# Attention and a mixture of experts in one kernel: sums of the first expert moved to GpSimd, and the tasks around the border of the two parts placed anew

## The chip, the cores and the metric

The kernel runs on one core of one Trainium2 chip. Its time is device microseconds of that core. A core has five engines that work side by side, each through its own queue of instructions in order: TensorE (PE, matrix multiplications into PSUM; PEld is its load of the stationary operand), VectorE (DVE), ScalarE (ACT), GpSimd (POOL) and SyncE (SP, which only issues DMAs here). They wait for each other through semaphores.

## The reference, cut to what matters

```python
def _attn_ref(q, k, v):                      # batch 8, heads 8, seq 576, head_dim 64
    scores = scale * np.matmul(q, k.transpose(0, 1, 3, 2))
    bias = slopes[:, None, None] * (-np.abs(rel).astype(np.float32))[None, :, :]
    mask = (rel >= 0) & (rel < window)       # window 128
    scores = np.where(mask, scores + bias[None], -1000000000.0)
    attn = np.exp(scores - np.max(scores, axis=-1, keepdims=True))
    attn = attn / (np.sum(attn, axis=-1, keepdims=True) + 1e-09)
    return np.matmul(attn, v)

def _moe_ref(x, w_gate, w1, w2):             # N 4608, D 512, E 8 experts, F 1024
    logits = x @ w_gate
    expert_idx = np.argmax(logits, axis=1)
    gate_w = softmax(logits)[arange(N), expert_idx]
    for e in range(E):                       # over the rows of expert e
        y[rows] = np.maximum(x[rows] @ w1[e], 0.0) @ w2[e]
    return gate_w[:, None] * y
```

The output of the attention, laid out as 4608 rows of 512, is the x of the second part. All is float32.

## The kernel before

**Attention.** The batch is cut into 4 pairs of sequences (bp) and each pair into 4 pairs of heads (hp): 16 units u. A unit has four groups g of key blocks (GR); the main loop runs over the 64 groups i. `scores(i)` (L762) makes a group's products on PE (L769), takes the exponential on ACT (L775) and multiplies with the bias factors on DVE (L778, L783); the result is `prob[i]`. `values` (L792, L804) multiplies it with v, `finish` (L812) copies the result into `xT` (L821, L823) and makes the sums of the softmax on PE (L836), which DVE adds to `sumT` (L847). A constant AHEAD = 3 sets how many groups the scores are ahead of the values. Loads of the unit after next are paced by small DMAs that wait for a `prob` (L640).

**Routing.** When a pair's four units are done, a list of tasks (`behind`, L1309) is worked off, one entry at each call of `some()` (one per group): `gate` and `turn` make the logits and bring tokens to partitions; `scale_a` to `scale_c` make the softmax scales, the choice of expert and `es`, the factor of each row and head (L952); `count` and `place` number the tokens of each expert (PE L967, L969); `ones_at`, `ones_at2` and `enlist` (L1000 to L1033) build the table of tokens through one-hot matrices. The rows, unscaled, and their scales go to `x_rows` in memory (`row_out`, or `squares_turned` and `squares_out` where DVE turns 32x32 squares; POOL puts the scales in, L1099, then DMAs, L1108). After the third pair, `early_table` numbers the first 512 tokens of expert 0, and `gather` (L1230, POOL) reads them back. The last pair's list is made by `with_tail` (L1607) and worked off inside the first layer of expert 0.

**Experts.** Groups run in a list: expert 0, expert 1, then further tiles and experts in turn. `prepare` (L1288) makes for each of an expert's four tiles a `to_scale` (DVE, L1252) and a `to_columns` (L1254; for experts 0 and 1 turned on PE, L1265, and copied by ACT, L1266), then sums. The two layers (`strassen1` L1415, `strassen2` L1496) use seven products M1 to M7 (ORDER: 1, 2, 6, 5, 7, 3, 4) in place of eight, each in two halves of 8 matmul records. M1 and M2 need no sums and only tiles 0 and 1; M6, M5 and M4 need sums of x (`xs`, four DVE instructions, L538 to L541) or of w1 (`ws`, L530 to L533); the second layer needs eight sums of w2 (`w2s`) and sums of the hidden layer (`hs`). After each half `step()` issues one entry of the list `fill`, so that list sets where the instructions of tasks stand on every engine, PE's queue among them. `drain(g)` issues what is left of a group's entries before its layer ends.

**The border.** In the last unit, expert 0's `prepare` is added to the tasks at its first group, so tiles 0 to 2 are scaled and turned inside the unit and tile 3 and the x sums just behind. `with_tail` has 13 entries. In expert 0's second layer stand the gather for expert 1, `count_all`, `check_all`, `table_further`, `next_groups` (values loaded from `xe` into registers) with `pieces` "1", `pieces` "2" (PE L1142, which waits for DVE's `index`), and then the whole of `prepare(fixed[1])`. The weights of expert 1 (L1587, L1588) go where the attention's rows lay, and so wait for the last DMAs out of them.

The lines that set how far the scores are ahead:

```python
        AHEAD = 3
        for i in range(AHEAD):
            scores(i)
...
            if i + AHEAD < NG:
                scores(i + AHEAD)
```

## Time and profile before

| what | us |
|---|---|
| median of 3 runs (731.38 to 735.25) | 732.21 |
| the profiled execution | 691.06 |
| its span, first to last instruction | 689.2 |
| mean granted TensorE clock | 0.985 |

Busy time by stage, from the view by stretches of time:

| stretch, us | what runs | PE busy | DVE busy | ACT busy | POOL busy | PE clock |
|---|---|---|---|---|---|---|
| 0 to 20 | first unit and a half | 11.86 | 8.90 | 9.80 | 17.09 | 1.00 |
| 168 to 181 | end of attention | 9.86 | 5.43 | 4.13 | 4.57 | 0.87 |
| 181 to 205 | expert 0, first layer, with the last pair's tasks | 23.36 | 17.96 | 7.61 | 1.33 | 1.00 |
| 205 to 220 | its end and the start of the second layer | 14.33 | 14.69 | 3.61 | 0.00 | 1.00 |
| 219 to 233 | second layer, M6 and M5 | 10.46 | 9.22 | 0.74 | 4.26 | 0.88 |
| 233 to 245 | second layer, M7 to M4 | 12.00 | 6.54 | 3.46 | 3.29 | 1.00 |

How to read it: an engine with less busy time than the stretch is long waited, or had nothing to do. PE is the only one that is nearly full over the whole span, so the question at each place is what PE waits for. In a timeline, the number in brackets is the idle time just before the instruction, and behind the arrow stands what ended it. A PE clock below 1.00 means that part of the stretch ran at half rate.

### The profile page before, as it was taken

What the parts mean: (1) busy time and instruction counts of PE and PEld (TensorE: products, weight loads), DVE (VectorE), ACT (ScalarE), POOL (GpSimd) and SP (SyncE); (2) the same over time, 40 slices, a digit from 0 to 9 for tenths busy, and PEclk for the clock granted to TensorE, in tenths of its full rate; (3) what the DMA queues carried; (4) which work ended last, traced back from release to release, by engine and by line L of the source; (5) the groups of instructions that cost most, each with busy time, mean ns of one, the idle gap of its engine ahead of it and who ended that gap; (6) DMA issues with size and microseconds to landing.
All of it is one profiled execution on the core that took longest, in us unless ns stands there. A gap on an engine that the chain in (4) does not pass through costs nothing.

```text
span 689.2 us, 14460 instructions
## 1 busy us (share of the span) xinstructions
PE 655.8 (95%) x6004; PEld 548.2 (80%) x6004; DVE 379.4 (55%) x717; ACT 199.2 (29%) x365; POOL 237.6 (34%) x360
## 2 busy tenths in 40 slices
PE   5899889998999899999999999999999999999996
PEld 4778768687687788878897887888788978878893
DVE  4567769786489476614842564275148435633500
ACT  5555446465331223113202310231131123002210
POOL 8100572215001176117323702652172247023020
PEclk9999899999999999999999999999999999999999
DMA  9677987854516964185448237652844573284010
GB/s 285 200 222 192 287 241 219 289 157 149 165 22 162 386 206 140 57 292 170 155 154 301 57 129 258 212 166 63 296 137 145 178 276 97 86 305 154 1 62 8
DMA packets 63549, 122.00 MB, mean 177 GB/s; under 512 B 5905, under 2 KB 30001, under 8 KB 63474
## 3 DMA queue, kind: packets, MB, share of 16 engines
q1 hardware_dynamic: 51778, 92.78, 42.0%
q0 software_dynamic: 10544, 27.31, 12.4%
q8 instruction: 49, 0.80, 0.5%
q10 hardware_dynamic: 1152, 0.88, 0.4%
q14 instruction: 26, 0.21, 0.1%
HBM read 101.79 MB, written 19.96 MB: 177 GB/s over the span
## 4 chain that ended last, share of the span: by engine, by line
PE 75%; issue 9%; DVE 8%; DMA 4%; POOL 2%; ACT 1%; SPq 0%; POOLq 0%; DVEq 0%; ACTq 0%
PE sp L769 5%; PE at L804 5%; PE pair0b L1511 4%; PE pair0a L1511 4%; PE pair0b L1454 4%; PE pair0a L1454 4%; PE pair1a L1511 4%; PE pair1b L1511 4%; PE pair2b L1454 4%; PE pair1b L1454 4%; PE pair1a L1454 4%; PE pair2a L1454 4%; PE pair2a L1511 4%; PE pair2b L1511 4%; PE m L836 3%
## 5 line engine op out<-in xcount | busy, mean ns | idle before, releaser
L1240 POOL DMA_INDIRECT xg<-x_rows,p_idx x124 | 125.0, 1008 | 37.8 <-issue 37.5
L1534 POOL DMA_INDIRECT out_dram<-zo,s_idx x39 | 44.5, 1140 | 250.6 <-DVE zo L1525 149.6
L769 PE MATMUL sp<-q_sb,k_sb 64*64 64x192 f32 (+2 forms) x1152 | 60.2, 331 | 7.1 <-DMA q_sb<-in_qT_dram 6.9
L775 ACT ACTIVATE pe<-sp 128x768 f32<-128x768 f32 x64 | 51.9, 811 | 49.6 <-PE sp L769 46.7
L804 PE MATMUL at<-pe,v_sb 64*64 64x192 f32 (+2 forms) x1408 | 59.6, 289 | 3.4 <-issue 3.4
L778 DVE TENSOR_TENSOR pe<-pe,fac 128x768 f32<-128x768 f32 x48 | 45.5, 952 | 28.3 <-ACT pe L775 27.8
L804 PEld LDWEIGHTS at<-pe,v_sb 64*64 64x64 f32 x1408 | 48.0, 138 | 9.5 <-issue 6.9
L769 PEld LDWEIGHTS sp<-q_sb,k_sb 64*64 64x64 f32 x1152 | 42.0, 141 | 16.6 <-DMA q_sb<-in_qT_dram 4.3
L1465 ACT ACTIVATE h<-h 128x512 f32<-128x512 f32 x32 | 20.2, 631 | 41.3 <-DVE h L1464 41.3
L836 PE MATMUL m<-pe,ind 128*32 128x192 f32 (+2 forms) x704 | 29.8, 288 | 0.6 <-issue 0.6
L1252 DVE TENSOR_TENSOR xn<-xg 128x512 f32<-128x512 f32 x39 | 26.3, 676 | 3.4 <-DMA xg<-x_rows,g_idx 3.1
L836 PEld LDWEIGHTS m<-pe,ind 128*32 128x32 f32 x704 | 23.2, 110 | 3.0 <-issue 1.0
L1108 POOL DMA_DIRECT2D x_rows<-xs x40 | 21.6, 548 | 6.4 <-POOL xs L1099 1.9
L783 DVE TENSOR_TENSOR pe<-pe,fac 128x768 f32<-128x768 f32 x16 | 15.3, 955 | 15.2 <-ACT pe L775 15.1
L1268 DVE STREAM_TRANSPOSE xgT<-xn 128x512 f32<-128x512 f32 x31 | 22.1, 712 | 1.1
L538 DVE TENSOR_TENSOR w2s<-w 128x512 f32<-128x512 f32 x16 | 10.9, 684 | 19.4 <-DMA w<-in_moe_w_dram 19.4
L1099 POOL COPY xs<-sq 128x16 f32<-128x16 f32 x10 | 2.6, 258 | 53.8 <-ACT sq L1081 53.8
L1566 PE MATMUL pair2a<-w,h 128*128 128x512 f32 x48 | 21.1, 592 | 0.0
L821 ACT COPY xT<-at 128x640 f32<-128x640 f32 (+1 forms) x32 | 18.7, 585 | 6.5 <-PE at L804 4.6
L1454 PE MATMUL pair0b<-xgT,w 128*128 128x256 f32 x72 | 17.2, 382 | 0.0
L1511 PE MATMUL pair1a<-w,h 128*128 128x256 f32 x72 | 17.0, 379 | 0.0
L1454 PE MATMUL pair0a<-xgT,w 128*128 128x256 f32 x72 | 17.0, 379 | 0.0
(375 smaller groups left out, 1393.2 us busy)
## 6 DMA issues: line engine op xcount, KB each, us to landing
w<-in_moe_w_dram SPq DMA_DIRECT2D x29, 2048.0 KB, 7.9
k_sb<-in_kT_dram SPq DMA_DIRECT2D x15, 576.0 KB, 5.6
q_sb<-in_qT_dram SPq DMA_DIRECT2D x15, 576.0 KB, 5.6
v_sb<-in_v_dram SPq DMA_DIRECT2D x30, 288.0 KB, 4.5
x_rows<-xs POOLq DMA_DIRECT2D x16, 264.0 KB, 3.8
x_rows<-xs POOLq DMA_DIRECT2D x32, 66.0 KB, 4.7
x_rows<-xT SPq DMA_DIRECT2D x8, 264.0 KB, 5.2
w<-in_moe_w_dram SPq DMA_DIRECT2D x4, 512.0 KB, 7.7
```

The source lines that it names most:

```text
L769: nc.tensor.matmul(sp[c * KB : (c + 1) * KB, r, c0 : c0 + n], lhsT=k_sb[u][hs, c, kb * KB : (kb + 1) * KB], rhs=q_sb[u][hs, c, kb * KB : k ...
L775: nc.scalar.activation(pe[:], sp[:, :, :GC], AF.Exp, scale=SCALE)
L778: nc.vector.tensor_tensor(pe.rearrange("p r (k c) -> p r k c", k=2), pe.rearrange("p r (k c) -> p r k c", k=2), fac[:, h0 : h0 + 2, None, ...
L804: nc.tensor.matmul(acc[r * D : (r + 1) * D, c, lo - q0 : hi - q0], lhsT=v_sb[u][c * KB : (c + 1) * KB, kb, r * D : (r + 1) * D], rhs=pe[c ...
L836: nc.tensor.matmul(sm[32 * j : 32 * j + 32, lo - q0 : hi - q0], lhsT=none[:] if pe is None else ind[:, hp, :], rhs=fac[:, 0, :KB] if pe is ...
L1108: eng.dma_start(x_d[r0 : r0 + n * m, a * PW : (a + 1) * PW].rearrange("(k i) w -> i k w", i=TQ), xs[a * TQ : (a + 1) * TQ, p0 // TQ : p0 / ...
L1240: nc.gpsimd.indirect_dma_start(out=to, out_offset=None, in_=where, in_offset=bass.IndirectOffsetOnAxis(ap=idx, axis=0),)
L1252: nc.vector.tensor_tensor(xn[:], x, s.unsqueeze(3).to_broadcast([P, NA, HP, TQ]), op=ALU.mult)
L1268: nc.vector.transpose(to.rearrange("p h (k j) -> p k h j", j=TQ), xn[:])
L1454: nc.tensor.matmul(ps[:, f * 256 : (f + 1) * 256], lhsT=left[m][:, d, fb * P : (fb + 1) * P], rhs=right[m][:, d, :], start=(m in (1, 2, 5) ...
L1511: nc.tensor.matmul(ps[:, :256], lhsT=left[m][:, f, c * P : (c + 1) * P], rhs=right[m][:, f, :], start=(m in (1, 2, 5) and f == 0), stop=Tr ...
L1534: ins = nc.gpsimd.indirect_dma_start(out=out[:, :], out_offset=bass.IndirectOffsetOnAxis(ap=s_idx[:, g["c0"] + j : g["c0"] + j + 1], axis= ...
```

## The change

It has five parts.

1. `scores_to` takes the place of AHEAD: two groups ahead in units 0 and 1, three from unit 2 on.
2. Expert 0: `prepare` is added to the tasks one group later, and only its first three entries (tile 0 scaled; tile 0 turned with tile 1 scaled; tile 1 turned with tile 2 scaled). The others, `first[3]` to `first[8]`, stand in `with_tail`: tile 2 is turned after M1's first half, tile 3 after its second. Expert 1 likewise: tiles 0 and 1 are turned in expert 0's second layer, tiles 2 and 3 and the x sums in its own first layer.
3. The four x sums of expert 0 and its eight w2 sums run on POOL, all placed after M1's second half; before, on DVE, the w2 sums spread over the second half of the first layer and the start of the second.
4. The last pair's tasks: `scale_a2` and `scale_b2` have entries of their own, `ones_at` and `ones_at2` come one half later, the one-hot columns are taken from `oc_of`, `squares_scaled` (POOL's copies) stands apart from `squares_out` and is done for all nine tiles at once, and tile 8 goes out through POOL's DMA queue and no longer through SP's.
5. The numbering of the third pair: `early_holes` apart and one entry earlier, the table and the gather with `enlist`. In the second layer `next_groups` and `pieces` "1" have entries of their own.

```diff
@@ -533,12 +533,12 @@
                 lambda: eng.tensor_tensor(s4, a12, s2, op=ALU.subtract),
             ]
 
-        def sums_t(b11, b12, b21, b22, t1, t2, t4):
+        def sums_t(b11, b12, b21, b22, t1, t2, t4, eng=nc.vector):
             return [
-                lambda: nc.vector.tensor_tensor(t1, b12, b11, op=ALU.subtract),
-                lambda: nc.vector.tensor_tensor(t2, b22, t1, op=ALU.subtract),
-                lambda: nc.vector.tensor_tensor(b12, b22, b12, op=ALU.subtract),
-                lambda: nc.vector.tensor_tensor(t4, b21, t2, op=ALU.subtract),
+                lambda: eng.tensor_tensor(t1, b12, b11, op=ALU.subtract),
+                lambda: eng.tensor_tensor(t2, b22, t1, op=ALU.subtract),
+                lambda: eng.tensor_tensor(b12, b22, b12, op=ALU.subtract),
+                lambda: eng.tensor_tensor(t4, b21, t2, op=ALU.subtract),
             ]
 
         def w1_sums(g, eng=nc.vector):
...
@@ -1080,23 +1080,29 @@
                 half = slice(r * KB, (r + 1) * KB)
                 nc.scalar.copy(sq[half].rearrange("p t k h -> p k t h"), ps5[half, :, :, r, :])
 
+        def squares(bp, t):
+            if (bp, t) not in xs_of:
+                if bp in spare and t < TPB - 1:
+                    w = NA * PW
+                    flat = spare[bp].rearrange("p h n -> p (h n)")
+                    xs_of[bp, t] = flat[:, t * w : (t + 1) * w].rearrange("p (k w) -> p k w", k=NA)
+                else:
+                    xs_of[bp, t] = rows.tile([P, NA, PW], F32, name="xs")
+            return xs_of[bp, t]
+
         def squares_turned(bp, t):
-            if bp in spare and t < TPB - 1:
-                w = NA * PW
-                flat = spare[bp].rearrange("p h n -> p (h n)")
-                xs = flat[:, t * w : (t + 1) * w].rearrange("p (k w) -> p k w", k=NA)
-            else:
-                xs = rows.tile([P, NA, PW], F32, name="xs")
-            xs_of[bp, t] = xs
+            xs = squares(bp, t)
             nc.vector.transpose(
                 xs[:, :, :PD].rearrange("p k (h j) -> p k h j", h=HP),
                 xT[bp][:, :, t * P : (t + 1) * P].rearrange("p h (k i) -> p k h i", k=NA),
             )
 
+        def squares_scaled(bp, t, n=1):
+
+            for k in range(t, t + n):
+                nc.gpsimd.tensor_copy(squares(bp, k)[:, :, PD:], sq_of[bp][:, k])
+
         def squares_out(bp, t, eng, n=1):
-
-            for k in range(t, t + n):
-                nc.gpsimd.tensor_copy(xs_of[bp, k][:, :, PD:], sq_of[bp][:, k])
             if n == 1:
                 xs = xs_of.pop((bp, t))
             else:
@@ -1149,7 +1155,7 @@
                 scalar1=float(NA), scalar2=K["piece"][:], op0=ALU.mult, op1=ALU.add,
             )
 
-        def early_table():
+        def early_holes():
 
             ps = ps_m.tile([P, 512], F32, name="m")
             nc.tensor.matmul(ps[:, :E], lhsT=K["ones"][:], rhs=acc[:], start=True, stop=True)
@@ -1157,6 +1163,8 @@
             nc.vector.tensor_scalar(hole[:], ps[:, 0:1], scalar1=-1.0, scalar2=float(CAP), op0=ALU.mult, op1=ALU.add)
             nc.vector.tensor_scalar_max(hole[:], hole[:], 0.0)
             nc.vector.tensor_tensor(K["off"][:, 0:1], K["off"][:, 0:1], hole[:], op=ALU.add)
+
+        def early_table():
             tok = rte.tile([P, NJ], F32, name="tok_0")
             number(tok[:], lambda k: parts[:, k, 0, :NJ])
             index(slice(0, NJ), tok[:], "0")
@@ -1267,12 +1275,16 @@
             else:
                 nc.vector.transpose(to.rearrange("p h (k j) -> p k h j", j=TQ), xn[:])
 
-        def x_sums(g):
+        def new_xs(g):
+            g["xs"] = mx_pool.tile([P, 3, 2, 256], F32, name="xs")
+
+        def x_sums(g, eng=nc.vector):
             x = g["xT"]
-            g["xs"] = mx_pool.tile([P, 3, 2, 256], F32, name="xs")
+            if "xs" not in g:
+                new_xs(g)
             o = g["xs"]
             return sums_t(
-                x[:, 0:2, :256], x[:, 0:2, 256:], x[:, 2:4, :256], x[:, 2:4, 256:], o[:, 0], o[:, 1], o[:, 2],
+                x[:, 0:2, :256], x[:, 0:2, 256:], x[:, 2:4, :256], x[:, 2:4, 256:], o[:, 0], o[:, 1], o[:, 2], eng,
             )
 
         def later(make, n):
@@ -1295,14 +1307,10 @@
             else:
                 todo = [[f, t] for f, t in zip(scales, cols)]
             if n == NJ:
-                sums = later(lambda: x_sums(g), 4)
+                sums = later(lambda: x_sums(g, nc.gpsimd if g is fixed[0] else nc.vector), 4)
                 if "ws" not in g:
                     sums += later(lambda: w1_sums(g), 8)
-                if g is fixed[1]:
-                    todo[-1].append(sums.pop(0))
-                    todo += [sums[k : k + 2] for k in range(0, len(sums), 2)]
-                else:
-                    todo += [[f] for f in sums]
+                todo += [[f] for f in sums]
             return [(g, t) for t in todo]
 
 
@@ -1319,16 +1327,19 @@
             )
             if bp == 0:
                 rt = [lambda t=t: squares_turned(bp, t) for t in range(TPB)]
-                ro = [lambda t=t: squares_out(bp, t, nc.gpsimd) for t in range(TPB)]
+                ro = [
+                    lambda t=t: (squares_scaled(bp, t), squares_out(bp, t, nc.gpsimd)) for t in range(TPB)
+                ]
                 return [g3[0:1], g3[1:2], g3[2:] + t3[0:1], t3[1:], a, a2 + rt[0:1], b + rt[1:2], b2 + rt[2:3],
                         c + n + rt[3:4], [], q + p, p2 + ro[0:4], o, o2, rt[4:6], e + rt[6:8] + ro[4:8]]
             rt, ro = ([lambda t=t, f=f: f(bp, t) for t in range(TPB)] for f in (row_turned, row_out))
             if bp == 1:
...
-            return [g3, t3, a + a2, b + b2 + rt[0:1], c + n + rt[1:2], rt[2:4], p + p2 + ro[0:4], o + o2 + rs[4:6], rs[6:9],
-                    e, [early_table, lambda: gather(fixed[0], x_d[: 3 * 2 * S, :])]]
+            return [g3, t3, a + a2, b + b2 + rt[0:1], c + n + rt[1:2], rt[2:4], p + p2 + ro[0:4], o + o2 + rs[4:6],
+                    rs[6:9] + [early_holes], e + [early_table, lambda: gather(fixed[0], x_d[: 3 * 2 * S, :])]]
 
         tasks = []
 
@@ -1338,9 +1349,14 @@
                     f()
 
         NG = 4 * len(units)
-        AHEAD = 3
-        for i in range(AHEAD):
-            scores(i)
+        scored = [0]
+
+        def scores_to(n):
+            while scored[0] < min(n, NG):
+                scores(scored[0])
+                scored[0] += 1
+
+        scores_to(2)
         route_consts()
         no_earlier_than(prob[0][0:1, 0, 0:1])
         load_v(1, 0, nc.sync)
@@ -1364,8 +1380,7 @@
                 values(u, 0, (4,))
                 finish(u, 0)
                 some()
-            if i + AHEAD < NG:
-                scores(i + AHEAD)
+            scores_to(i + (3 if u < 2 else 4))
             if u in (10, 11):
                 ws_tasks.pop(0)()
             if g == 0:
@@ -1379,8 +1394,9 @@
             else:
                 values(u, 1, (6, 7, 8))
                 finish(u, 1)
-            if u == len(units) - 1 and g == 0:
-                tasks.extend(t for _, t in prepare(fixed[0]))
+            if u == len(units) - 1 and g == 1:
+                first = [t for _, t in prepare(fixed[0])]
+                tasks.extend(first[:3])
             if g != 2:
                 some()
             if g == 3 and hp == HP - 1 and bp < BP - 1:
@@ -1413,6 +1429,8 @@
         ORDER = ((1, 0), (2, 1), (6, 0), (5, 2), (7, 0), (3, 2), (4, 0))
 
         def strassen1(g, start=None):
+            if "xs" not in g:
+                new_xs(g)
             w, x, ws, xs = g["w1"], g["xT"], g["ws"], g["xs"]
             hf = F // 2
             left = {1: w[:, 0:2, :hf], 2: w[:, 2:4, :hf], 3: ws[:, 2], 4: w[:, 2:4, hf:], 5: ws[:, 0], 6: ws[:, 1],
@@ -1432,6 +1450,7 @@
                 o = g["w2s"]
                 more += sums_t(
                     w2[:, a, :256], w2[:, a, 256:], w2[:, b, :256], w2[:, b, 256:], o[:, 0, a], o[:, 1, a], o[:, 2, a],
+                    nc.vector if start is None else nc.gpsimd,
                 )
             if start is None:
                 fill.extend((g, [f]) for f in more)
@@ -1602,26 +1621,25 @@
                     seq.append(fixed[2 + x])
             groups[:] = seq
 
-        self_late = []
-
         def with_tail(g, w2s):
 
             bp = BP - 1
             spare[bp] = xp.tile([P, HP, 2 * S], F32, name="xT")
             rt = [lambda t=t: squares_turned(bp, t) for t in range(TPB)]
-            ro = [lambda: squares_out(bp, 0, nc.sync, 4), lambda: squares_out(bp, 4, nc.sync, 4), lambda: squares_out(bp, 8, nc.sync)]
-            w = [[f] for f in w2s]
-            a, b, p, o = (
-                [lambda f=f, f2=f2: (f(bp), f2(bp))]
-                for f, f2 in ((scale_a, scale_a2), (scale_b, scale_b2), (place, place2), (ones_at, ones_at2))
-            )
-            c, n, q, e = ([lambda f=f: f(bp)] for f in (scale_c, count, scales_squared, enlist))
+            ro = [lambda: squares_out(bp, 0, nc.sync, 4), lambda: squares_out(bp, 4, nc.sync, 4), lambda: squares_out(bp, 8, nc.gpsimd)]
+            o = [lambda: ones_at(bp), lambda: ones_at2(bp)]
+            p = [lambda: place(bp), lambda: place2(bp)]
+            a, a2, b, b2, c, n, q, e = (
+                [lambda f=f: f(bp)]
+                for f in (scale_a, scale_a2, scale_b, scale_b2, scale_c, count, scales_squared, enlist)
+            )
             todo = [
-                [lambda k=k: gate(bp, k) for k in range(3)] + rt[0:1], [lambda k=k: turn(bp, k) for k in range(3)] + rt[1:2],
-                a, rt[2:3], b, rt[3:4], c + n, rt[4:5] + w[0], q + p + ro[0:1] + rt[8:9], rt[5:6] + o, rt[6:8] + ro[2:3],
-                ro[1:2] + w[1] + w[2], e + w[3], [table_fixed] + w[4] + w[5],
+                first[3] + [lambda k=k: gate(bp, k) for k in range(3)],
+                first[4] + first[5] + first[6] + first[7] + first[8] + w2s + [lambda k=k: turn(bp, k) for k in range(3)]
+                + rt[0:1], a, a2 + rt[1:2], b, b2 + rt[2:3], c + n + rt[3:4], rt[4:5] + rt[8:9],
+                q + p + [lambda: squares_scaled(bp, 0, TPB)] + ro[0:1] + ro[2:3], rt[5:7], o + rt[7:8] + ro[1:2], [], e,
+                [table_fixed],
             ]
-            self_late.extend(w[6] + w[7])
             return [(g, t) for t in todo]
 
 
@@ -1635,14 +1653,15 @@
             if i == 0:
                 strassen1(g, start=with_tail)
                 end_of_tail()
-                fill.append((g, [lambda: gather(fixed[1], x_d[:, :]), self_late[0]]))
-                fill.append((g, [self_late[1], count_all]))
-                fill.append((g, [check_all]))
-                fill.append((g, [table_further]))
-                fill.append((g, [next_groups, lambda: pieces(slice(NJ, E * NJ), "1")]))
-                fill.append((g, [lambda: pieces(slice(E * NJ, NC), "2")]))
-                fill.extend(prepare(fixed[1]))
+                todo = [t for _, t in prepare(fixed[1])]
+                sums = [f for (f,) in todo[9:]]
+                now = [
+                    [lambda: gather(fixed[1], x_d[:, :])], [count_all], [check_all], [table_further], [next_groups],
+                    [lambda: pieces(slice(NJ, E * NJ), "1")], [lambda: pieces(slice(E * NJ, NC), "2")],
+                ] + todo[:3] + [sums[k : k + 2] for k in range(0, len(sums), 2)]
+                fill.extend((g, t) for t in now)
                 strassen2(g)
+                fill.extend((None, t) for t in [todo[3], todo[4], todo[5] + todo[6], todo[7] + todo[8]])
                 w_of = lambda k: (w1_a, w2_a) if k % 2 == 0 else (lp["w"], lp["w"])
                 load_w1(groups[2], w1_a)
                 load_w2(groups[2], w2_a)
```

## The prediction

> **What bounds the kernel now.** I read the page's engine shares and its chain first, then the timeline of PE for the stretches where PE isn't full, then DVE and POOL beside it.
>
> ```profile
> PE 655.8 (95%) x6004; PEld 548.2 (80%) x6004; DVE 379.4 (55%) x717; ACT 199.2 (29%) x365; POOL 237.6 (34%) x360
> PE 75%; issue 9%; DVE 8%; DMA 4%; POOL 2%; ACT 1%; SPq 0%; POOLq 0%; DVEq 0%; ACTq 0%
> ```
>
> PE is the bound; from 233 us on it has no idle time until the last matmul. So the change can be worth only what PE loses before 233 us. The places it touches, in PE's timeline:
>
> ```profile
> 10.31 0.84 PE L804 MATMUL at<-pe,v_sb 64*64 64x192 f32 x16
> 13.04 0.88 PE L769 MATMUL sp<-q_sb,k_sb 64*64 64x192 f32 x16 [1.89 <-DMA q_sb<-in_qT_dram]
> ...
> 172.72 0.66 PE L1265 MATMUL m<-ident,xn 128*128 128x128 f32 x4 [2.48 <-DVE xn L1252]
> ...
> 175.95 2.22 PE L804 MATMUL at<-pe,v_sb 64*64 64x64 f32 x48
> ...
> 180.20 0.63 PE L1265 MATMUL m<-ident,xn 128*128 128x128 f32 x4 [0.65 <-DVE xn L1252]
> 180.66 1.89 PE L1454 MATMUL pair0a<-xgT,w 128*128 128x256 f32 x8
> ...
> 220.68 1.13 PE L1511 MATMUL pair1a<-w2s,hs 128*128 128x256 f32 x4 [1.35 <-DVE w2s L539]
> ...
> 226.61 1.03 PE L1142 MATMUL m<-ta,to_squares 128*128 128x7 f32 x8 [2.19 <-DVE tb L1131]
> 227.50 2.72 PE L1511 MATMUL pair0a<-w2s,hs 128*128 128x256 f32 x8
> 230.01 2.88 PE L1511 MATMUL pair0b<-w2s,hs 128*128 128x256 f32 x8
> ...
> 244.84 1.89 PE L1454 MATMUL pair2a<-xgT,w 128*128 128x256 f32 x8
> ```
>
> The reader is to see a wait in brackets, and behind two of them matmuls that run at half speed: 48 attention matmuls take 2.22 us (24 took 0.84 at 166.59), eight layer matmuls 2.72 and 2.88 (otherwise 1.89, 1.73 from start to start). DVE is what PE waits for here; it is busy 14.69 of the 15 us from 205 to 220.
>
> ```profile
> 158.67 1.35 DVE L1015 TENSOR_TENSOR gsr<-cols_b,rc 128x1152 bf16<-128x1152 bf16 x1
> ```
>
> ```profile
> 158.69 1.38 POOL L1053 COPY xs<-es 128x16 f32<-128x16 f32 x1
> ...
> 160.90 0.21 POOL L1053 COPY xs<-es 128x16 f32<-128x16 f32 x1
> ```
>
> A copy of POOL that takes 0.21 us alone took 1.38 beside a two-input DVE instruction, and ended with it.
>
> **What the Trainium skill says.** SBUF — State Buffer, Who interferes with whom: a DVE instruction with two SBUF inputs and a GpSimd instruction that reads SBUF exclude each other, and the second waits for the whole first. The three lines above agree for GpSimd as the second; for DVE as the second the trace has only GpSimd instructions too short to tell. GPSIMD Engine Reference, 3.1 Elementwise: about 2.6 cycles per element for a two-input operation, 4497 ns for 2048. TensorE: Matmul & The Clock Gate, Part 1: after an idle window of about 3.4 us the array runs at half rate for at least another; the slow matmuls above fit, and here an idle time of 1.7 to 2.5 us was enough.
>
> **The start.** Two groups of scores instead of three stand ahead, so one group's values, the values of block 4 and the first sums (24+8+24 matmuls, 13.71 to 15.40 without the scores between: 1.7 us) come before the scores of unit 1, which wait for q until 13.04. Three groups' scores end near 9.0, so this work fits into 9 to 12.5. Gain 1.7; bounds 0 (exponentials now late for unit 1: the chain of ACT 0.81 and DVE 0.96 has some 2.2 us of PE work as cover) and 1.9.
>
> **The end of attention** (times on the clock of before). The gather isn't earlier: it starts at 167.98 when the last x_rows writes (issued to 164.56, some 3.3 us each) have landed, whatever the table does. But only tiles 0 and 1 are turned before the first layer, and the first comes one slot later, behind finish. PE gets there at 171.45, waits to 172.72 (1.3 instead of 2.48), finishes attention at full clock, tile 1 ends at 175.8, ACT's copy (0.59) lets M1 start at 176.5 instead of 180.66. Two turnings (0.43 each) now follow M1's halves: net 3.3. The gates' wait (0.35) goes too. Tile 3's copy is done near 184.1, M2 ends near 188.2.
>
> **DVE's load.** Twelve sums of 0.68 us, 8.2 in all, go to POOL. With these off DVE, the w2s wait (1.35) and the wait for the second pieces (2.19, also put one block later) go, and with them the half clock behind (5.22 for two blocks of 1.73: 1.8). What is late next without any contention: ones_at now stands behind M3's first add and two transposes, enlist two blocks later; 3.0 us of one-hots end some 1.1 us after PE wants them. In expert 1 tile 3's turning, ACT's copy, M2's add and two sums (0.69 each) end 0.5 after M6 could start. Eight x_rows DMAs of SP (5.43 us of issue) go to POOL's queue, behind which only the gather stands; the landing that releases expert 1's w1 and the gather comes about 4 us earlier, w1 (4 MB with w2 at 310 GB/s: 14 us) before it is needed. Sum without contention: 1.7 + 3.3 + 0.3 + 3.5 + 1.8 - 1.1 - 0.5 = 9.0 us gained.
>
> **The sums on POOL.** No such instruction is in the trace. Estimate from the skill's 4497 ns: 512 elements in 1.15 to 1.2 us; with the semaphore and start between two of them some 1.35. Twelve from 184.1 end near 200.5. M6 needs the second x sum by 188.2: it is there near 186.7. strassen2 needs w2s long after. But DVE has to reach es (L952) by 197.0, when PE wants it behind M7's first half. In before DVE took from 190.42 to 198.86 for it without a pause; here it starts at 186.7, so es would be ready at 195.3, with a cover of only 1.7 us. In that stretch stand 17 two-input instructions (four L889, L896, two L910, L919 to L921, L930 to L935, L941, L952). If each waits behind a sum, one or sometimes two get through per sum: by 200.5 twelve or thirteen are done, and es comes near 202. The bounds: no delay, and 17 x 1.35 = 23 us, which the end of the twelve sums cuts to about 10. I take a delay that leaves PE idle for some 4.6 us at L1073, plus 1.4 for the half clock behind: 6.0 lost of 9.0. Net gain 3 us.
>
> **The sum.** The profiled execution took 691.06 us with a span of 689.2; it becomes 688 with a span of 686. The median shown is 732.21, 41 us above; nothing in the profile says where these lie, so I carry the difference over as it is: 729.2, say 729.
>
> **Rivals.**
> 1. No mutual exclusion worth the name: POOL takes its operands while DVE runs on, or in bursts. For it: a POOL cast at 18.37 and a DVE product at 18.51 overlapped, and the product took its usual 0.96. Against it: the 1.38 us copy. Then the full 9 us: 723.
> 2. Slower: the sums hold DVE so long that es is the new bound. Same place (DVE between L889 and L952), price 12 us for each us by which a sum and its gap exceed 1.35; it decides from about 1.6 us, where the idle time at L1073 reaches some 7.5 and eats everything. At 2 us a sum they end at 208, PE is idle for 12 and the sum is 5 us worse: 737. For it: a first sum on POOL that also has to wait for DVE's instructions between; against it: two inputs at 2.6 cycles don't make 2 us.
> 3. The change doesn't reach PE's early stretch: the saved 1.7 us at the start is given back at the next instruction or v_sb wait (65.6 to 67.0 shows 1.42). That takes 1.7 off any case; for it, such gaps stand at fixed instructions, so they move along, which speaks against.
>
> **How the numbers follow.** Forecast (exclusion, some 6 us lost) 0.42, by itself 725 to 734; rival 1 0.32; rival 2 0.26; rival 3 is a shift inside each. 0.5% is 3.7 us and is what the measurement can tell from no change. The forecast lies near that bound, so it gives some 0.17 to faster and 0.21 to no change, 0.04 to slower; rival 1 all to faster; rival 2 0.02 to no change, the rest to slower. Faster 0.49, same 0.23, slower 0.28. The range from 721 (all gains, and the clock kept up) to 737 leaves out the far ends of rivals 1 and 2.
>
> **What would show it.** Right: first scores of unit 1 at about 13 with sums ahead of them; M1 some 6 us earlier (4.2 and the start); POOL sums of 1.2 to 1.4 us; DVE's short two-input instructions far apart between 185 and 200; an idle time of PE before L1073; no wait before the pieces. Wrong: es on time (rival 1), or an idle time there above 8 us (rival 2); a first sum on POOL of several us; w1 of expert 1 landing after M1 wants it.

## The result, and the profile after

The changed kernel took 739.95 us (median of 13 runs, 735.33 to 750.79) beside 731.92 for the kernel before (13 runs, 723.30 to 736.73) on the same chip: ratio 1.0148, 95% interval 1.0105 to 1.0191. The forecast was 729, its range 721 to 737: a gain of 3 us was expected and a loss of 8 came. Medians here are over all runs, while the ratios leave out slow runs (more than 1.5% above the fastest of the same kernel), so a ratio can differ from that of the two medians.

The profiled execution of the changed kernel took 744.94 us, 5 above its median and within its runs. That of before, from which the prediction was made, took 691.06, far under every one of those 13 runs. So the two profiles can't simply be set side by side; a second profile of before is among the experiments.

The page of after, busy time of PE and the chain of waits:

```profile
PE 677.3 (91%) x6004; PEld 559.3 (75%) x6004; DVE 378.6 (51%) x705; ACT 196.5 (26%) x365; POOL 254.6 (34%) x380
PE 62%; issue 15%; DVE 6%; another core or an unknown queue 5%; POOL 5%; DMA 2%; ACT 2%; ACTq 0%; SPq 0%; POOLq 0%; DVEq 0%
```

PE has as many records as before, and waits more. "Unknown queue" is new in the chain. PE's timeline of after shows where. (Names pair0a to pair2b are PSUM buffers, a and b for the two halves of a product. The same code has other line numbers in each kernel: L1454 of before is L1473 of after.)

```profile
178.34 1.99 PE L1473 MATMUL pair0a<-xgT,w 128*128 128x256 f32 x8 [0.68 <-ACT xgT L1274]
...
197.22 1.96 PE L1473 MATMUL pair0a<-xgT,w 128*128 128x256 f32 x8
205.34 1.96 PE L1073 MATMUL m<-es,to_squares 128*128 128x72 f32 x8 [6.16 <-DVE es L952]
...
207.90 3.76 PE L1473 MATMUL pair0b<-xgT,w 128*128 128x256 f32 x8
211.45 2.81 PE L1473 MATMUL pair2a<-xgT,ws 128*128 128x256 f32 x8
...
255.96 1.97 PE L1473 MATMUL pair2a<-xs,ws 128*128 128x256 f32 x8 [0.55 <-issue]
...
264.66 1.89 PE L1473 MATMUL pair2b<-xgT,w 128*128 128x256 f32 x8
279.54 3.78 PE L1473 MATMUL pair1a<-xgT,ws 128*128 128x256 f32 x8 [12.99 <-DVE h L1495]
```

M1 starts at 178.34 (180.66 before). The waits for w2s and for the second pieces are gone. The wait for `es` at L1073 is there, as forecast, with half clock behind it (3.76 for a half that takes 1.89). Then, in expert 1, come 13 us of waiting before M3 that the prediction does not have.

Three lengths tell the kernels apart: M1's start; the tail, from M1 of expert 0 to the first matmul of expert 1; and the period from one expert's first matmul to the next one's. They are read from the start times of these matmuls. "Held" is explained with the first experiment. All runs in one table, medians of the timed runs beside those of the kernel before in the same series of runs:

| run | held | M1 at | tail | expert 1 | experts 2 to 6 | median us, before | ratio (95%) |
|---|---|---|---|---|---|---|---|
| before, first profile | no | 180.7 | 64.2 | 62.5 | 62.5 | | |
| after, first profile | yes | 178.3 | 69.1 | 79.9 | 68.1 to 70.4 | 740.0, 731.9 | 1.0148 (1.0105, 1.0191) |
| before_again | yes | 180.6 | 64.2 | 68.0 | 68.0 to 70.4 | 729.0, 730.0 | 0.9997 (0.9968, 1.0025) |
| after_again | yes | 177.6 | 68.9 | 79.3 | 68.0 to 70.3 | 742.1, 730.0 | 1.0218 (1.0148, 1.0288) |
| e1_before | yes | 175.8 | 69.6 | 68.4 | 67.9 to 70.6 | 729.7, 730.0 | 1.0059 (1.0021, 1.0097) |
| w2s_late | yes | 173.0 | 65.4 | 79.8 | 66.4 to 68.7 | 735.6, 730.0 | 1.0135 (1.0073, 1.0197) |
| combined | yes | 181.2 | 66.4 | 70.2 | 67.9 to 70.3 | 730.1, 732.7 | 0.9983 (0.9954, 1.0012) |
| burst_later | yes | 176.8 | 68.9 | 74.6 | 68.4 to 69.9 | 741.5, 732.7 | 1.0177 (1.0148, 1.0206) |
| two_halves | little | 178.2 | 64.2 | 62.5 | 64.3 to 64.5 | 701.2, 732.7 | 0.9617 (0.9583, 0.9651) |
| plain_copies | no | 180.6 | 64.2 | 62.5 | 62.5 | 688.1, 732.7 | 0.9420 (0.9382, 0.9459) |
| after_halves | little | 176.5 | 69.2 | 64.2 | 64.2 to 64.3 | 705.4, 727.9 | 0.9735 (0.9684, 0.9786) |
| combined_halves | little | 179.4 | 66.3 | 62.5 | 64.2 to 64.3 | 700.8, 727.9 | 0.9638 (0.9583, 0.9694) |
| start_halves | little | 176.2 | 64.2 | 62.5 | 64.2 to 64.3 | 698.9, 727.9 | 0.9654 (0.9598, 0.9709) |
| sums_dve_halves | little | 175.7 | 66.1 | 64.2 | 64.2 to 64.3 | 702.7, 727.9 | 0.9691 (0.9629, 0.9753) |
| before_delay | no | 178.7 | 64.2 | 67.0 | 62.5 | 694.1, 688.4 | 1.0088 (1.0061, 1.0115) |
| start_parts | no | 181.3 | 64.2 | 62.5 | 62.5 | 690.8, 688.4 | 1.0042 (1.0021, 1.0063) |
| combined_parts | no | 173.0 | 67.7 | 62.5 | 62.5 | 690.5, 688.4 | 1.0038 (1.0010, 1.0065) |
| before_delay9 | no | 179.0 | 64.2 | 64.5 | 62.5 | 693.1, 688.4 | 1.0075 (1.0042, 1.0108) |
| after_third | no | 174.9 | 69.0 | 64.2 | 62.5 | 691.6, 688.4 | 1.0044 (1.0019, 1.0069) |
| start_only | no | 181.0 | 64.2 | 62.5 | 62.5 | 687.3, 688.4 | 0.9984 (0.9960, 1.0008) |

The last two series (three rows each) fell where the kernel before takes 688 us (41 and 33 runs, 683 to 697), the others where it takes 728 to 733 (718 to 743). The runs of one series share a chip. So there are two kinds of chip, or two states of a chip, and by their lengths the prediction's profile came from the one, the times shown with it from the other. The chips are numbered, and number 2 stands at a series of each kind (730.0 and 688.4): if it is the same chip, a state of it decides. Below, "a chip with held signals" stands for either.

### The profile page after: what moved, and what is told of

The parts are those of the page before. It is cut to its first block, busy times and chain, and to the rows that moved or that the text cites. A ratio compares the mean times of both kernels' runs of the same rounds, so it can differ in the third digit from the quotient of the medians.

```text
span 743.2 us, 14471 instructions
## 1 busy us (share of the span) xinstructions
PE 677.3 (91%) x6004; PEld 559.3 (75%) x6004; DVE 378.6 (51%) x705; ACT 196.5 (26%) x365; POOL 254.6 (34%) x380
## 3 DMA queue, kind: packets, MB, share of 16 engines
q0 software_dynamic: 10800, 27.58, 12.1%
## 4 chain that ended last, share of the span: by engine, by line
PE 62%; issue 15%; DVE 6%; another core or an unknown queue 5%; POOL 5%; DMA 2%; ACT 2%; ACTq 0%; SPq 0%; POOLq 0%; DVEq 0%
PE sp L769 6%; PE at L804 5%; PE pair1a L1530 3%; PE pair0a L1530 3%; PE pair0b L1530 3%; PE pair1b L1530 3%; POOL xg L1248 3%; PE pair0b L1473 3%; PE pair2a L1530 3%; PE pair2a L1473 3%; PE pair2b L1530 3%; PE pair2b L1473 3%; PE m L836 3%; PE pair1a L1473 2%
## 5 line engine op out<-in xcount | busy, mean ns | idle before, releaser
L1248 POOL DMA_INDIRECT xg<-x_rows,p_idx x124 | 123.1, 993 | 37.8 <-issue 37.5
L804 PE MATMUL at<-pe,v_sb 64*64 64x192 f32 (+2 forms) x1408 | 61.1, 294 | 2.2 <-issue 2.1
L778 DVE TENSOR_TENSOR pe<-pe,fac 128x768 f32<-128x768 f32 x48 | 45.7, 954 | 26.9 <-ACT pe L775 26.7
L1114 POOL DMA_DIRECT2D x_rows<-xs x48 | 26.0, 549 | 6.7 <-POOL xs L1103 3.0
L1530 PE MATMUL pair1b<-w,h 128*128 128x256 f32 x72 | 18.2, 381 | 5.1 <-issue 5.0
L1530 PE MATMUL pair2b<-w,h 128*128 128x256 f32 x56 | 16.9, 438 | 4.7 <-issue 4.7
L1530 PEld LDWEIGHTS pair1b<-w,h 128*128 128x128 f32 x72 | 13.6, 190 | 8.3 <-issue 6.7
```

The lines of the kernel that those rows point to most:

```text
L778: nc.vector.tensor_tensor(pe.rearrange("p r (k c) -> p r k c", k=2), pe.rearrange("p r (k c) -> p r k c", k=2), fac[:, h0 : h0 + 2, None, ...
L804: nc.tensor.matmul(acc[r * D : (r + 1) * D, c, lo - q0 : hi - q0], lhsT=v_sb[u][c * KB : (c + 1) * KB, kb, r * D : (r + 1) * D], rhs=pe[c ...
L1114: eng.dma_start(x_d[r0 : r0 + n * m, a * PW : (a + 1) * PW].rearrange("(k i) w -> i k w", i=TQ), xs[a * TQ : (a + 1) * TQ, p0 // TQ : p0 / ...
L1248: nc.gpsimd.indirect_dma_start(out=to, out_offset=None, in_=where, in_offset=bass.IndirectOffsetOnAxis(ap=idx, axis=0),)
L1530: nc.tensor.matmul(ps[:, :256], lhsT=left[m][:, f, c * P : (c + 1) * P], rhs=right[m][:, f, :], start=(m in (1, 2, 5) and f == 0), stop=Tr ...
```

## The experiments

**before_again.** No edit.

> The kernel before, unchanged, to see a second profile of it. Theory A (a hold): in the changed kernel's profile PE's done signals come up to 12 us late and then in bursts 0.09 us apart, once in every expert, near the end of each burst of 20 gathers on POOL; the profile of before that the prediction read had none, and its timed runs are 41 us longer than it. Then this profile shows the same hold in every expert, a period of 68 to 69 us from expert to expert instead of 62.5, and a span near 730. Theory B (the change makes the hold): the profile looks as the first one, period 62.5, span near 690, and the 41 us stay unexplained.

Theory A. The span is 727.9 and every expert takes 68 to 70 us. ACT's timeline of before_again, the copies of M7's halves (L1474), and PE's:

```profile
260.51 0.59 ACT L1474 COPY u<-pair2a 128x512 f32<-128x512 f32 x1 [4.65 <-PE pair2a L1454]
...
265.38 0.59 ACT L1474 COPY u<-pair2b 128x512 f32<-128x512 f32 x1 [2.89 <-PE pair1a L1454]
```

```profile
260.26 1.89 PE L1454 MATMUL pair2b<-xgT,w 128*128 128x256 f32 x8
...
266.74 1.99 PE L1454 MATMUL pair1b<-xgT,ws 128*128 128x256 f32 x8 [2.87 <-DVE h L1476]
```

M7's first half ends near 260.4, and its copy starts at 260.51. The second half ends by its record at 262.15, and its copy starts only at 265.38. In the trace's semaphore records PE's done signals of this stretch are missing at their times and then come several at once, 0.09 us apart (275.94, 276.04, 276.13 and 276.22). That is what "held" means. It happens in every expert beside the burst of 20 gathers that GpSimd issues from 2.7 us after the expert's first matmul (247.4 to 272.8 here), and ends some 3 us behind it. Whether PE's work or only its signal is late can't be told, as the profile models the ends of matmuls. This execution took 729.79 us, 38.7 more than the one that the prediction was made from (691.06), and the six periods of experts 1 to 6 are 38.8 us longer in sum (5.5 to 7.9 each): the whole difference lies there.

**after_again.** No edit.

> The changed kernel, unchanged, for its ratio on this chip and a second profile. Theory A: ratio 1.010 to 1.019, es late at L1073 by some 6 us again (it follows from the order of the work), the hold somewhere in each expert again, of a size that differs from run to run. Theory B: the 13 us before M3 of expert 1 are there again in the same place and size.

The wait for es and a hold in each expert came again as theory A has it (the ratio, 1.0218, lies above its range), but the 13 us before M3 of expert 1 are there again in place and size (12.97), as theory B said. So something in the changed kernel's order makes the hold costlier in expert 1: 79.3 against 68.0. ACT's timeline of the first profile of after shows the same:

```profile
261.18 0.58 ACT L1491 COPY u<-pair2b 128x512 f32<-128x512 f32 x1 [2.59 <-remote]
278.18 0.59 ACT L1493 COPY u<-pair2a 128x512 f32<-128x512 f32 x1 [16.41 <-remote]
```

M7's first half ends at 264.83 by PE's record; ACT gets its signal at 278.10, and that of the second half at 278.19. The burst began at 249.9. M3 needs the add (L1495) behind this copy, and so waits for the whole hold.

**e1_before.** The changed kernel, expert 1 prepared as before:

```diff
-] + todo[:3] + [sums[k : k + 2] for k in range(0, len(sums), 2)]
+] + todo[:4] + [todo[4] + todo[5]] + [sums[k : k + 2] for k in range(0, len(sums), 2)]
 strassen2(g)
-fill.extend((None, t) for t in [todo[3], todo[4], todo[5] + todo[6], todo[7] + todo[8]])
```

(`sums` starts at `todo[6]` here.)

> The changed kernel with expert 1 prepared as in the kernel before: all four tiles turned, and its x sums done, ahead of or beside its first layer's start. Theory A (the loss lies in the tail, between 200 and 215 us): the time stays within 3 us of the changed kernel's, the 0.5 us at M6 of expert 1 go. Theory B (the later turning of expert 1 puts its first layer beside the gathers in such a way that M3 waits 13 us): the 13 us go, and the time falls by 8 to 17 us, to or under that of before.

Expert 1 takes 68.4 us again and the time falls by 12.4 us to 729.7; by the ratio, 1.0059, it stays a little over before. PE's timeline of e1_before: the wait for es is still there, that before M3 is a short one at its second half.

```profile
202.82 1.96 PE L1073 MATMUL m<-es,to_squares 128*128 128x72 f32 x8 [6.16 <-DVE es L952]
...
266.76 3.57 PE L1473 MATMUL pair1b<-xgT,ws 128*128 128x256 f32 x8 [2.20 <-issue]
```

Theory B was right on what costs most on this chip: the later turning of expert 1.

**w2s_late.** `w2s` leaves the second entry of `with_tail` for the tenth:

```diff
-first[4] + ... + first[8] + w2s + [lambda k=k: turn(bp, k) for k in range(3)]
+first[4] + ... + first[8] + [lambda k=k: turn(bp, k) for k in range(3)]
...
-q + p + ... + ro[2:3], rt[5:7], o + rt[7:8] + ro[1:2], [], e,
+q + p + ... + ro[2:3], rt[5:7] + w2s, o + rt[7:8] + ro[1:2], [], e,
```

> The changed kernel with the eight w2s sums of the first expert still on GpSimd, but four blocks later, behind the scales' work on DVE. Theory A (the twelve sums keep DVE from es, PE waits 6.2 us at L1073 and then runs at half clock, some 5 us): that wait falls under 1.5 us and the half clock behind it goes, 8 to 10 us gained against the changed kernel, less what the sums take from DVE later (1 to 4 us: the one-hots of L1015 stand there). Theory B: the wait at L1073 isn't what decides, the time stays within 3 us.

PE's timeline of w2s_late:

```profile
203.25 0.56 PE L1025 MATMUL m<-oc,gsr 128*128 128x96 bf16 x9 [1.01 <-DVE gsr L1015]
217.41 1.04 PE L1148 MATMUL m<-ta,to_squares 128*128 128x24 f32 x8 [1.00 <-DVE ta L1133]
222.80 1.03 PE L1148 MATMUL m<-ta,to_squares 128*128 128x7 f32 x8 [2.53 <-DVE tb L1137]
...
270.46 3.78 PE L1473 MATMUL pair1a<-xgT,ws 128*128 128x256 f32 x8 [12.95 <-DVE h L1495]
```

No wait at L1073 any more; the tail falls from 68.9 to 65.4, and part of the gain is given back to waits for the pieces. The 13 us stay. The time falls by 6.5 us, more than the tail alone gives. So there are two losses, not one.

**combined.** Both edits.

> The changed kernel with both of the edits of the last runs: expert 1 prepared as before, and the eight w2s sums on GpSimd four blocks later. If the two losses are separate and add (theory A: es late by 6 us in the tail, and 11 us in expert 1 by the hold), the tail from M1 to expert 1's first layer takes some 66 us (before 64.2), expert 1's period is 68 to 69, and the time is 0 to 4 us under before, 16 under the changed kernel. If they are one loss that moves (theory B), the 13 us wait or the wait for es is back in another place and the time stays above before.

They add: tail 66.4, expert 1 70.2, 730.1 us, no different from before (0.9983). With the two losses cut to 2.2 us each (64.2 and 68.0 before), what is left of the change is worth nothing that can be measured.

**burst_later.** The changed kernel; in expert 1 the gathers stand behind the turning of its last tile, with a one-element copy of that tile on GpSimd ahead of them:

```diff
-for a in ahead:
-    gather(a, x_d[:, :])
+def burst(late=ahead, g=g, hold=(i == 1)):
+    if hold:
+        ...
+        nc.gpsimd.tensor_copy(touch[:], g["xT"][0:1, 0, 511:512])
+    for a in late:
+        gather(a, x_d[:, :])
...
+if i == 1:
+    fill[1] = (None, fill[1][1] + [burst])
+else:
+    burst()
```

> The changed kernel, with only the 20 gathers that GpSimd issues beside expert 1's first layer moved 2.6 us later, behind the turning of its last tile. Theory A (a cliff in time: PE's done signals are held from 13 to 14.5 us after the first gather of a burst, and M7's first half ends at 14.5 in the changed kernel, at 12.7 in before): M7's signal now ends at 11.9 and passes, the wait of 13 us before M3 goes, expert 1's period falls from 79.5 to 68 to 73, and the time by 7 to 11 us. Theory B (the later turning itself, its place in PE's and DVE's order, makes the wait): the period stays at 79 or more.

PE's timeline of burst_later:

```profile
266.76 1.99 PE L1473 MATMUL pair1a<-xgT,ws 128*128 128x256 f32 x8 [1.96 <-DVE h L1495]
...
274.49 3.78 PE L1473 MATMUL pair1b<-xgT,ws 128*128 128x256 f32 x8 [5.73 <-issue]
```

The 13 us became 1.96 and 5.73, and expert 1 takes 74.6 us; but the profiled execution is the shortest of this kernel's six runs, and the ratio, 1.0177, lies between the two of the changed kernel. A half answer: the place of the burst matters, but the sharp edge in time that theory A names isn't shown.

**two_halves.** The kernel before; of each burst 8 gathers at once, 12 behind M7's first copy:

```diff
-    gather(a, x_d[:, :])
+    gather(a, x_d[:, :], range(1))
+g["mid"] = lambda a=ahead[-1]: gather(a, x_d[:, :], range(1, NJ))
...
 nc.scalar.copy(u3[:, c, :], ps[:])
+if c == 0 and "mid" in g:
+    nc.gpsimd.tensor_copy(touch[:], u3[0:1, 0, 0:1])
+    g["mid"]()
```

> The kernel before, with each burst of 20 gathers cut in two: 8 at once, 12 behind M7's first copy, with some 3 us without a gather between. Theory A1 (the hold comes from 13 us of gathers without a pause): no hold, or one only at the very end of the second part; expert periods fall from 68 towards 62.5 and the time by 20 to 40 us. Theory A2 (the hold depends on the end of the gathers alone, or on something else): held signals as before or later, period 68 to 72, time 0 to 25 us longer.

POOL's timeline of two_halves: the pause.

```profile
317.02 0.94 POOL L1241 DMA_INDIRECT xg<-x_rows,p_idx  x1 [0.30 <-issue]
321.37 0.18 POOL L1478 COPY touch<-u 1x1 f32<-1x1 f32 x1 [3.40 <-ACT u L1475]
322.03 0.96 POOL L1241 DMA_INDIRECT xg<-x_rows,p_idx  x1 [0.48 <-issue]
```

A pause of 4 us in the gathers brings 31.5 us: 701.2, ratio 0.962. Signals still come late near the end of the second part: the second half of the second layer's M1 ends at 332.78 by PE's record, and ACT's copy of it starts at 339.21. From expert 2 on 1.8 to 2.0 us per expert are lost to this.

**plain_copies.** Each indirect gather of the pieces becomes a DMA of 128 consecutive rows:

```diff
-nc.gpsimd.indirect_dma_start(out=to, out_offset=None, in_=where, in_offset=...)
+nc.gpsimd.dma_start(out=to, in_=where[:P, :])
```

> The kernel before, with the gathers of the pieces (experts 2 to 7 and the further groups) replaced by plain copies of 128 consecutive rows, issued by GpSimd in the same places: it leaves out the choice of rows. Theory A (indirect gathers cause the hold): no held signals, period 62.5, time near 690. Theory C (the hold comes from something else at that place, the weights' loads or PE itself): the hold stays, period 68, time near 730.

Stretches of experts 1 and 2, of before_again and of plain_copies (length, busy time of PE, PEld, DVE, ACT, POOL with counts, PE's clock, DMA share, GB/s):

```profile
244.70:312.70 68.00, 63.40 (x306) 52.48 (x305) 36.41 (x60) 12.02 (x24) 26.47 (x26) 1.00 0.49 161
312.70:382.60 69.90, 66.16 (x305) 54.12 (x304) 31.18 (x51) 12.11 (x24) 25.81 (x25) 0.95 0.48 159
```

```profile
244.80:307.30 62.50, 62.50 (x305) 52.59 (x305) 36.72 (x60) 12.34 (x24) 17.70 (x26) 1.00 0.51 176
307.30:369.80 62.50, 62.50 (x305) 52.59 (x304) 31.39 (x51) 12.55 (x24) 16.69 (x25) 1.00 0.53 177
```

With plain copies PE is busy 62.50 of 62.50 us on a chip where the kernel before takes 732.7. So the gathers make the hold, not the weights' loads or PE, nor the amount that is moved (161 GB/s over 68.00 us and 176 over 62.50 are about the same bytes). The copies are also shorter (16.7 us of POOL in place of 25.8), so it isn't shown whether the indirection or the length of the burst does it.

**after_halves, combined_halves, start_halves, sums_dve_halves.** The cut of two_halves on the changed kernel, on combined, on the kernel before with the start alone, and on the changed kernel with `nc.vector` for all twelve sums.

> The changed kernel with its gathers cut in two as in the run before, so that the change is read without the hold. Theory A (the change loses in two places: some 5 us in the tail by GpSimd's sums, 11 in expert 1 by the hold, and gains 3 to 5 up to M1): expert 1's period is 63 to 65, and the time 0 to 4 us over that of the kernel before with cut gathers (701.2, ratio 0.962), so a ratio of 0.962 to 0.967. Theory B (the later turning of expert 1 loses by itself): expert 1's period stays over 70, and the ratio is over 0.975.

> Cut gathers, with the changed kernel's start and first expert, but expert 1 as before and the w2s sums four blocks later. Theory A: 1 to 4 us under the kernel before with cut gathers (701.2), ratio 0.956 to 0.961: the best of all so far. Theory B: no better than it, 0.962 or more.

> The kernel before with cut gathers and, of the change, the start alone (two groups of scores ahead in the first two units). The prediction's step: 1.7 us gained, bounds 0 and 1.9; the last scores of the attention stand 1.9 us earlier in the changed kernel's profile. So 699.3, ratio 0.959. Its rival: given back at the next wait of the attention stage, 701 and 0.962.

> The changed kernel with cut gathers and all twelve sums on DVE, in the same places of the program. Theory A (GpSimd's sums delay es by holding DVE, as the twelve cost DVE 7.5 us themselves: each needs 0.6 to 0.7 there against 1.27 on GpSimd): es comes about as late, PE waits 4 to 7 us at L1073, and the time is within 2 us of the one with the sums on GpSimd: for es it is all the same who does them at this place. Theory B (mutual exclusion is the larger loss): the wait at L1073 falls under 3 us and the time by 3 us or more.

These ran in another series than two_halves, so they are compared with each other and by their periods. after_halves: expert 1 64.2, without the 13 us; so that wait needs both the later turning and the burst. The ratio, 0.9735, is over the range expected, though the lengths are those of theory A. By the medians the change costs 6.5 us against its start alone (705.4, 698.9); combined_halves (700.8) isn't told from start_halves, and its ratio falls where theory B put it. The start's 1.7 can't be read from this.

sums_dve_halves went against my theory A. PE's timeline:

```profile
200.22 1.08 PE L1073 MATMUL m<-es,to_squares 128*128 128x72 f32 x8 [2.90 <-DVE es L952]
```

The wait is 2.90, not 6.15 as in after_halves, and the tail 66.1, not 69.2. In the same places, the sums done by GpSimd delay DVE by more than the sums done by DVE itself. (In the timed runs the difference, 2.7 us, is within the scatter.)

**before_delay and before_delay9.** The kernel before, with idle matmuls in PE's queue ahead of M6 of expert 1:

```diff
+if m == 6 and g is fixed[1]:
+    for n in range(20):
+        nc.tensor.matmul(tp[:, ...], lhsT=ident[:], rhs=ident[:], start=True, stop=True)
```

> The kernel before, in which PE does 20 idle matmuls of 128x128 (about 2.2 us, into a tile that nobody reads) ahead of M6 of expert 1: M7's first half then ends some 14.8 us after the first gather of the burst, as in the changed kernel, against 12.7 before; nothing of the change itself is in it. Theory A (a cliff in time): a wait of 10 to 13 us appears before M3 of expert 1, its period goes from 68 to 78 to 80, and the time up by 8 to 12 us. Theory B (the later turning itself makes the wait): the period goes up by the 2.2 us alone, to 70, and the time by 2.

> The kernel before with 9 idle matmuls of 128x128 ahead of M6 of expert 1. The run with 20 of them took 4.5 us for them (two passes each), and fell on a chip on which the kernel before takes 688 us and shows no held signal at all; 9 are 2.0 us, the changed kernel's shift. On a chip with held signals, theory A (a cliff in time): a wait of 10 to 13 us before M3 of expert 1, its period 78 to 80, the time 8 to 12 us longer. Theory B (the later turning itself): period 70, 2 us longer. On a chip without them both say: period 64.5, 2 us longer.

Both fell on chips without a hold (twenty took 4.5 us, nine 2.0 in the period), and so say nothing on the edge. That question stays open. The median of before_delay9 is 4.8 us longer, though, for 2.0 in the profile: a difference of 2 to 3 us between two medians is not by itself proof of a cause.

**start_parts and combined_parts.** A third part: the last 4 gathers behind M1 of the second layer.

> The kernel before with the change's start and the 20 gathers cut in three (8 at once, 8 behind M7's first copy, 4 behind M1 of the second layer). If the length of a burst without a pause makes the hold, the second part (10 us instead of 14) makes none either: periods of experts 2 to 6 fall from 64.3 to 62.5, 1.8 each, and the time by some 9 us against the same with two parts (ratio 0.9654): 0.953. If what is left at 64.3 comes from elsewhere, the ratio stays at 0.962 to 0.967; a wait of DVE for the last tile could cost 1 to 2 us per expert.

> The same cut in three on the kernel with the change's start and first expert, expert 1 as before and the w2s sums later. Same expectation for the periods; against start_parts it shows what the rest of the change is worth without the hold: the tail from M1 to expert 1 takes 66.3 there against 64.2, and M1 comes up to 2 us earlier or not at all, so 0 to 2 us slower than start_parts.

Also without a hold: all periods 62.5 with three parts. What a third part is worth where signals are held isn't known. The cut brings nothing here, and start_parts is 0.4% slower than before for a reason that its profile doesn't show.

**after_third and start_only.** The changed kernel, and the start alone.

> The changed kernel on this chip. On a chip without held signals (the kernel before at 685 to 693 us): no 13 us wait, expert 1's period 63 to 64, the tail 69, and what is left of the change: +4.7 in the tail, +0.5 to 1.5 in expert 1, -1 to -3 up to M1, so 2 to 5 us slower, ratio 1.003 to 1.008. On a chip with them: 1.010 to 1.022 as so far.

> The kernel before with the change's start alone. The prediction's step: 1.7 us gained, a ratio of 0.9975 on either kind of chip. Its rival (the gain is lost again to idle times of the attention stage that fall into another place, and the half clock behind them): 0.999 to 1.003; the run with three parts of gathers hints at this, with M1 at 181.3 and half-clock time at 95 us.

after_third is the cleanest reading of the change: 691.6 against 688.4, 1.0044, within what was expected (expert 1, 64.2, is just over it). PE's timeline of after_third, the first matmul of M1, the wait for es, M6 of expert 1:

```profile
174.93 1.99 PE L1473 MATMUL pair0a<-xgT,w 128*128 128x256 f32 x8 [0.68 <-ACT xgT L1274]
...
201.95 1.96 PE L1073 MATMUL m<-es,to_squares 128*128 128x72 f32 x8 [6.15 <-DVE es L952]
...
252.43 1.97 PE L1473 MATMUL pair2a<-xs,ws 128*128 128x256 f32 x8 [0.54 <-DVE xs L539]
```

The start alone: 0.9984, with an interval that holds both 1 and 0.9975.

## Why the prediction was wrong, point by point

**The step that failed first is the carried difference.** "Nothing in the profile says where these lie, so I carry the difference over as it is." The second profile of before has 38.7 of these 41 us as held signals beside the bursts of gathers, and the change moves work into exactly that stretch: by turning tiles 2 and 3 of expert 1 inside its first layer it makes expert 1 take 79.3 to 79.9 us in place of 68.0. Undoing this one part gave 12.4 us back. The prediction priced this part at 0.5 us (M6 waits 0.55: right by itself), and no line of its one profile shows the rest. But this step is not the only one: where no signal is held the change still loses 3.3 us in place of gaining 3, by the next two steps.

**The wait for es: right mechanism, size too small.** Forecast were 4.6 us of idle time (its own times, 202 less 197.0, give 5.0) and 1.4 for the half clock, 6.0 in all. Measured are 6.15 to 6.16 us of idle time in each of the six profiles in which GpSimd's sums stand there. In the first one PE is at half clock from 203.1 to 213.3, and busy from 205.34 on:

```profile
205.34:213.30 7.96, 7.96 (x25) 6.88 (x26) 5.16 (x16) 1.91 (x5) 4.05 (x15) 0.50 0.31 64
```

(length, busy time of PE, PEld, DVE, ACT, POOL with counts, PE's clock, DMA share, GB/s). 7.96 us at half clock are 4.0 us of work lost, so the wait cost 10.2 in all. The profile of after, GpSimd's sums:

```profile
186.12 1.27 POOL L538 TENSOR_TENSOR xs<-xgT 128x512 f32<-128x512 f32 x1 [14.33 <-ACT xgT L1274]
187.47 1.27 POOL L539 TENSOR_TENSOR xs<-xgT,xs 128x512 f32<-128x512 f32 x1
...
200.29 1.47 POOL L541 TENSOR_TENSOR w2s<-w,w2s 128x512 f32<-128x512 f32 x1
```

DVE beside them in after, then the same lines in before_again:

```profile
189.34 3.28 DVE L889 TENSOR_TENSOR s<-gsr 128x32 f32<-128x32 f32 x4
192.66 1.16 DVE L895 TENSOR_SCALAR low<-s 128x72 f32<-128x72 f32 x1
...
196.48 2.72 DVE L910 TENSOR_TENSOR pr<-gsr,r 128x288 f32<-128x288 f32 x2
...
204.96 0.23 DVE L952 TENSOR_TENSOR es<-r,gw 128x72 f32<-128x72 f32 x1
```

```profile
190.92 0.53 DVE L889 TENSOR_TENSOR s<-gsr 128x32 f32<-128x32 f32 x4
191.49 0.20 DVE L895 TENSOR_SCALAR low<-s 128x72 f32<-128x72 f32 x1
...
192.76 0.82 DVE L910 TENSOR_TENSOR pr<-gsr,r 128x288 f32<-128x288 f32 x2
...
198.52 0.23 DVE L952 TENSOR_TENSOR es<-r,gw 128x72 f32<-128x72 f32 x1
```

The estimate for a sum (1.15 to 1.2 us, 1.35 with its gap) met 1.25 to 1.27 us for nine of the twelve and 1.36 to 1.47 for the last three, 1.22 to 1.44 from start to start. From L889 to the end of es DVE took 15.85 us (7.83 in before_again). That the sums on GpSimd do this, and not the new order, is seen in sums_dve_halves, where DVE does them first and then needs 7.82 us for the same stretch:

```profile
192.25 0.52 DVE L889 TENSOR_TENSOR s<-gsr 128x32 f32<-128x32 f32 x4
...
199.84 0.23 DVE L952 TENSOR_TENSOR es<-r,gw 128x72 f32<-128x72 f32 x1
```

DVE began as forecast: M2's add, ahead of L889, starts 10.4 us behind M1 (188.74), 10.2 in the forecast. But es ended 26.9 us behind M1, not 25.5: when the last sum ended (201.76) DVE had done eight of the two-input instructions and was ending the ninth, where the forecast had twelve or thirteen. (Its list has 15 of them, not 17.) The half clock is the larger miss, 4.0 us for 1.4: 10.2 us at half clock followed this idle time in five of the six profiles and 6.8 in e1_before, and 3.4 followed the one of 2.19 in before.

In this the Trainium skill's SBUF — State Buffer, Who interferes with whom, is borne out with GpSimd as the first of the two: the DVE instructions wait for whole sums. The section also names tensor_scalar, which can run in a two-port mode; L895 is a tensor_scalar (1.16 us against 0.20), and the prediction's list of two-input instructions left it out. RECIPROCAL, with one input, took 0.59 in both. Rival 2's place was right, its condition (1.6 us a sum) was not met, and it wasn't needed.

**Up to M1: about half of it.** Forecast 1.7 for the start and 4.16 for M1's place, 5.9. after_third has nearly all of it (M1 at 174.9, 5.7 earlier), and two runs at 173.0 more; in the mean it is half: eleven profiles with the change's start and end of attention have M1 at 176.6 (173.0 to 181.2), six without either at 179.6, three with the start alone at 179.5 (176.2, 181.0, 181.3). So in the mean the start alone gained nothing up to M1, as rival 3 has it, though three profiles with such scatter don't decide it. Two things are seen to take gain away. Idle times of the attention stage move when the start moves, and a half-clock window of 3.4 us in which PE is busy costs 1.7: start_only has one of 6.8 at 92.3, at a wait for `gs` (L861) of 4.69 us that is 1.44 in before. In the first profile of after such a window (172.3 to 175.7) lies on the very matmuls that the prediction saw "at full clock". And in five of the eleven (after, after_again, burst_later, combined, combined_halves), all on chips with held signals, PE has six idle times of 0.2 to 0.4 us, without a cause in the profile, beside expert 0's four gathers: M1 comes at 178.7 there in the mean, at 174.8 in the other six, which have none to three such times. Why only there isn't shown.

**The waits that should go** (w2s, second pieces) went in every profile of after, as did that for the gates. **Sum without a hold:** -3.0 up to M1, +4.8 in the tail (69.0 against 64.2), +1.7 in expert 1: 3.5 slower, measured 3.3. For tail and expert 1 together the forecast was 2.9 longer (5.6 gained by waits and clock; 6.0 for es, 1.1 for enlist, 0.9 for two turnings and 0.5 at M6 lost) and 6.5 were measured, 3.6 more. The wait for es cost 4.2 more, and the one for enlist's one-hots (L1025) 0.8 less (0.28 us in after_third for 1.1), which leaves 0.2. **With a hold:** expert 1 adds 11.3 in place of 1.7, so 13 slower; measured 8.0 and 12.1 as differences of medians (10.8 and 15.8 by the ratios).

Open are why signals are held on one kind of chip and not on the other, from which moment of a burst on, whether PE's work or only its signal is late, and whether delay alone makes the 13 us.

## What to carry to other kernels

When a profiled execution is far from the timed runs, get a profile that isn't, before pricing a change: the missing time has a place, and a change can land in it. An engine that is idle isn't free to take work if it shares its access to SBUF with the one that is late; put its share where nothing due soon stands on the other engine (w2s_late: no wait for es, and a tail of 65.4 us for 68.9). And when signals come late beside a long, unbroken burst of gathers, try cutting it: with one pause of 4 us the kernel before gains 3.8% where its signals are held, more than the whole change was meant to bring. Where they aren't, a cut in three, with the change's start, was 0.4% slower.

## What the runs showed of the hardware that was not expected

PE's done signals beside 20 back-to-back indirect gathers (25 us) came up to 13 us late and then in bursts 0.09 us apart; this cost 5.5 to 7.9 us per expert in before_again and nothing in the first profile of before, the same program. The length of an idle time of PE does not fix what follows: 6.16 us were followed by 10.2 us at half clock in after and by 6.8 in e1_before, 2.90 in sums_dve_halves by 6.8 as well.
